# Attention with product features and a multiplicative FFN on one core: the end of the first query quarter in halves, the first keys' maximum in three parts, and a new order of all steps

## The chip, the core and the metric

One core of a Trainium2 chip runs the whole program: TensorE (PE) multiplies, VectorE (DVE), ScalarE (ACT) and GpSimd (POOL) do the rest, and SyncE (SP) issues nearly all DMAs, ACT a few. The metric is the device time of one execution in microseconds.

## The reference

For 4 batches of 4 heads with 1088 rows of 32 numbers, keys and queries are mapped to 64 products each (8 sketches times 8 sketches), attention is computed without a softmax, and its 4352 rows of 128 numbers go through a feed-forward block with two products multiplied:

```python
def phi(x):
    a = np.einsum('rd,bhsd->bhsr', S1, x)
    b = np.einsum('rd,bhsd->bhsr', S2, x)
    return np.einsum('bhsi,bhsj->bhsij', a, b).reshape(*x.shape[:-1], r * r)
q_p, k_p = (phi(q), phi(k))
kv = np.einsum('bhsf,bhsd->bhfd', k_p, v)
z = np.sum(k_p, axis=2)
num = np.einsum('bhsf,bhfd->bhsd', q_p, kv)
den = np.einsum('bhsf,bhf->bhs', q_p, z)[..., None] + 1e-06
...
x = attn_out.transpose(0, 2, 1, 3).reshape(B * S, H * D)
a = x @ w1
b = x @ w2
h = a * b @ w3
out = h @ w_out
```

The sketches and the FFN weights arrive as 64-bit floats and are converted on the chip from their two words. `w3 @ w_out` is formed once ("fold"), so the last two products become one.

## The kernel before

The program is a set of named steps, each a small function that issues one or a few instructions, and a hand-written string `ORDER` that says in which order they are called. Each engine executes its own instructions in that order, so `ORDER` is the queue of every engine at once, SP's and ACT's DMA queues among them. `POOL` and `ACTS` name the steps that run on POOL or ACT where a choice exists; otherwise they run on DVE. `SLOTS` says which buffer of a kind each allocation takes, in the order of the allocations; an allocation waits until its buffer's last user is done.

The steps by their prefixes:

- `s.*`: the two sketches: loaded (`s.load`), put together from their words on ACT (`s.words`), scaled (`s.pair`) and split into a coarse part and a rest (`s.lead`, `s.sum`, `s.rest`), transposed, spread.
- `k0` to `k3`: the keys of one batch: loaded, their maximum (`max`, L569) gives a grid (`g`), on which they are split in `lead` and `rest`; `gram` forms their Gram matrix on PE; `Gm` to `N1` derive bounds and products from it, `ab` the sketches of the keys, `kp` their 64 products, `kv` the sums with the values; `kq` and `kz` bring these into the form that the queries use. `kr0`, `kr1` are the last 64 rows of two batches each. `v*.load` loads the values.
- `q0` to `q6`, `qr`: queries. `q0` and `q1` are the first two blocks of 512 rows, `q2` and `q3` the next two, `q4` and `q6` blocks of 1024, `qr` the 256 last rows of the batches. A block is transposed (`tr`), split, multiplied with the sketches (`A0`, `C0`, `A1`, `C1`), its products corrected (`sm`, `st`, `sh`, `sl`, `sc`), the denominators formed (`p01`, `p2`, `p12`, `dn`, `de`, `rc`), the products written out (`phi`), transposed on PE or DVE (`pt`, `pT`), multiplied with `kz` or `kq` (`x`) and copied to `xT`, the FFN's input. Only `q0` divides at the very end: `xs` (L1198) multiplies with the reciprocals, `xt` (L1206) transposes on PE, `xT` (L1213) copies on ACT.
- `w0` to `w10`: weights: loaded, and converted from words by ACT (`c`, `m`), DVE (`j`) and POOL (`a0`, `a1`). `w0` is the first half of the columns of w1 and w2, `w1` the second, `w2` is w_out, the rest are row blocks of w3. `f*` folds one block of w3 with w_out.
- `g0` to `g7`, `gr`: the FFN of 512 rows (`gr`: the 256 last): for each of 8 column blocks c a product with w1 (`a`, L1448), its copy on ACT (`c`, L1453), a product with w2 (`b`, L1458), their product on DVE (`m`, L1464), and the accumulation with the folded weights (`o`, L1471; for `gr` in two banks `o0`, `o1`, L1478). Then the result is brought back (`oT`) and stored (`st`): four stores on SP for each of g0 to g7 (L1426), one on ACT (`gr.st0`) and one on SP (`gr.st1`) for `gr` (L1432).
- `warm*`: matmuls of zeros that nobody reads (`idle_ps`, L221), 72 in all, and `c.act`, a copy of one number on ACT early on.

PE's instructions stand as `ORDER` has them. Near the end, the last group's accumulations alternate between the two banks, with `gr.oT0` and `gr.st0` ahead of the last of the second bank.

Of the kernel before, what the change touches and what calls it, by code (L numbers as in the profile page):

```python
# [66 lines left out]
k1.lead0 k1.tr1 warm23 q0.A0 warm15 w1.load kr0.ab warm4 warm12 kr0.abc k1.rest0 q1.l2 warm13 warm7 warm18 q0.C0 k0.N0
kr0.kp w1.m v0.load q0.sma q0.C0t q0.sta k0.N1 k0.kv0 k0.kv3 k1.gram0 k1.gram1 k0.kv1 q1.l1 k0.kv2 kr1.load v0.loadr
k0.kvr s.RC k0.Na warm10 warm21 kr1.tr k0.kvc k0.kvm q0.sha q0.sla k0.Nb k2.zero k0.Nh w0.load warm17 k1.tr0 kr1.kT
q0.sca k1.kT1 k1.kT0 k0.kzt q1.A0 k0.kz q0.A1 kr1.ab q0.al q0.phi0 q0.phi1 q1.sm q0.smy q0.sty q1.st q0.pt0 warm5  # L70
k0.kqt k0.Nl warm20 k0.Nf w0.m kr1.abc q0.pc0 q0.pt1 q0.shy q1.rm q0.C1 k1.gram2 k1.gram3 k1.gram4 q0.pc1 warm19 q0.x0
q1.load k0.Nr q0.sly q0.C1t q0.x1 w0.c q0.scy q0.p01 q0.p2 q1.sh q0.p12 q0.dn s.KS w0.j q1.C0 q0.de q1.sl q0.rc q0.xs
q0.xt q0.xT k1.ab w0.a1 v1.zero k2.load k2.loadr k2.max w1.c warm24 w0.a0 warm22 g0.3a q1.sca q1.p01 g0.3c k2.g
v1.loadr k1.Gm k2.lead0 q1.scy q1.al w2.load q1.p2 q1.p12 k1.abt q1.restT q1.dn g0.1a g0.3b w1.j q1.de k0.kq q1.rc
k1.Gt g0.3m q1.bs g0.2b w1.a0 q1.phi g0.0a g0.5a g0.4a q1.pt0 g0.0c w2.c g0.1c w3.load w2.m k2.rest0 q1.pt1 g0.6a
g0.2a q1.pc0 w2.j k1.Ga k1.kp0 q1.pc1 g0.5c g0.2c g0.6c k2.gram0 q2.tr k1.Gb k1.T0 k2.gram1 k1.T1 q2.max k1.Ta k1.Tb
k1.Ts w2.a0 w4.load q1.x w1.a1 k2.gram2 k2.gram3 k2.gram4 k1.N0 k1.N1 s.AR warm16 k2.Gm q1.xT g1.7a q2.l2 k2.Gt k2.Ga
g0.6b g0.0b w3.c q2.l1 k1.Na k1.Nb k1.Nr k2.Gb w4.m g0.4c g0.6m g0.1b g0.7a g0.0m q2.rm w4.c q2.C0 q2.A0 q2.C1 g0.1m
w4.j w3.j g1.7c warm28 g0.7c w3.m g1.4a g1.2a g0.7b q3.tr q2.Ct g0.2m g1.6a q2.At g1.6c w4.a0 w3.a0 g1.1a g1.7b
q2.load q3.max q4.tr w6.load v1.load w2.a1 w4.a1 g1.2c f1.t g0.7m w3.a1 g1.1c w6.c q3.l2 g1.5a g1.7m q3.l1 q2.sm f0.t  # L80
g1.3a g0.4b f1.m w9.load warm27 f0.m q2.st q2.sh q4.max f0.o q2.sl g1.5c g0.4m q2.sc f1.o g1.3c g1.2b q2.p01 q3.rm
v2.zero k1.kp1 q2.al q2.p2 q2.p12 g1.2m k1.kv0 k2.T0 k1.kv2 k1.kv3 k2.T1 k1.kv1 k1.kvr q3.C0 q3.A0 q3.C1 w5.load
k1.kvc g1.4c k1.kqt k2.Ta k2.Tb q2.dn k2.Ts q2.de w6.j q2.rc g1.0a q3.Ct q2.bs g1.3b g1.6b g1.5b g1.3m q2.phi0 q3.At
w6.m g0.5b w5.m w5.c g1.5m g1.1b g1.0b g1.6m q3.sm g0.0o w9.c k1.kq w9.m g0.1o g1.0c k2.N0 k2.N1 q2.pT0 g0.5m q2.x0
g1.0m q3.st g1.1m q2.restT warm11 k3.zero w6.a0 k2.Na q3.sh w7.load kh2.load w6.a1 q3.sl w9.j k2.Nr w5.j q2.xT0 g1.4b
w9.a0 w9.a1 w5.a0 f3.t g1.0o q3.load g2.6a w10.load k3.loadr g2.6b g1.1o g2.1a g2.6c q4.l2 q4.l1 w7.m g2.1c w7.c g2.6m
g1.4m k2.Nb f6.t f3.m q3.sc g2.3a g2.7a g2.7c f3.o g2.3c q3.p01 q3.al k2.kT1 w5.a1 q3.p2 q3.p12 q3.dn k2.kT0 q4.rm
f6.m f6.o w10.c w8.load k2.ab w8.c q4.C0 q4.A0 q4.C1 w7.j k2.abt warm9 g2.4a f2.t q4.Ct g1.6o g2.0a f2.m g2.2b k3.load
q4.At q4.sm q3.de w7.a0 g2.0c f2.o v2.loadr w7.a1 kh3.load g0.2o f4.t q3.rc w10.m f4.m g2.2a k2.kp0 g0.6o f4.o q3.bs
w8.m w8.j g1.3o w8.a0 v2.load q3.phi0 g2.2c g2.4c w10.j q3.pT0 q3.x0 w8.a1 g0.3o q3.xT0 g2.7b w10.a0 w10.a1 k2.kp1  # L90
f5.t k3.max q6.tr f5.m g3.0b k3.kT1 g2.7m q3.restT f7.t g3.0a f5.o g3.0c g3.0m g3.3a g0.5o g3.3c g2.1b g2.2m g3.4a
g1.4o g1.5o k3.kT0 q6.max k3.g g2.1m g3.4c g2.5b f7.m f7.o g1.2o g2.0b q4.st q4.sh k3.lead0 q4.sl g3.7a g1.7o g3.7c
k3.rest0 kr1.kp q4.sc q4.al k2.kv0 k2.kv3 k2.kv1 k2.kv2 k3.ab k2.kvr k3.gram0 k3.gram1 k3.gram2 k3.gram3 k3.gram4
k2.kvc q4.p01 k2.kqt q4.p2 g2.0m k3.abt k3.Gm g0.4o g2.5a q4.p12 g2.5c k2.kq q4.dn q4.de k3.Gt g2.5m g3.6b g2.4b g2.0o
g3.6a q4.rc g3.6c k3.Ga q4.bs g1.oT g2.4m q4.phi0 q4.phi1 q4.pT0 k3.Gb g0.7o g3.4b g3.4m v3.zero k3.kp0 v3.load
v3.loadr g3.3b g2.4o g2.3b g2.3m g3.6m q4.pT1 g0.oT qr.max g3.2a g3.1a g2.6o g2.5o g3.2b g2.3o g3.3m k3.kp1 g3.1c
g3.2c qr.l2 k3.T0 k3.T1 k3.Ta g3.2m q4.x0 q4.x1 k3.kv0 k3.kv1 k3.Tb k3.N0 k3.kv3 k3.kv2 k3.kvr k3.Ts q6.l2 q6.l1 k3.N1
q6.rm k3.Na q4.xT0 warm6 k3.Nr k3.Nb q4.xT1 g4.2a g2.2o g5.2a g4.2c q6.C0 q6.A0 k3.kvc q6.C1 g5.2c q6.At q6.Ct q6.sm
k3.kqt g2.1o g4.3a g3.0o g5.4a g4.0a g2.7o g5.3a q6.st g4.0c g5.4c g5.3c g4.3c q6.sh q6.sl g5.0a q6.sc q6.p01 q6.al
q6.p2 q6.p12 g5.3b g2.oT g5.3m q6.dn g5.4b g5.7a q6.de k3.kq q6.rc qr.l1 qr.rm q6.bs q6.phi0 q6.phi1 g5.4m g5.1a  # L100
q6.pT0 g3.1b g5.1c g3.5a g5.7b g3.5c g5.0c g5.7c g3.1m q6.pT1 g3.4o g3.5b g3.3o q6.x0 q6.x1 q6.xT1 q6.xT0 g5.1b g5.7m
g5.1m g3.5m g5.0b g6.6a g3.7b g5.0m g3.7m qr.C0 g6.6c qr.A0 qr.C1 qr.At warm25 g6.0b g6.0a g6.0c g6.0m qr.Ct qr.sm
g5.2b g7.4a g4.1a g6.5a g4.4a g4.4c g4.1c qr.st qr.sh qr.sl g3.1o g5.2m g7.2a g3.6o g3.2o g4.5a g3.5o g4.5c g7.2c
g7.0a g4.4b g5.0o g5.1o g5.5a g5.2o g7.0c g7.4c g5.5c g6.2a qr.sc g4.4m qr.al g7.6a g6.4a g6.2c g6.5c g6.4c g5.6a
qr.p01 g5.6c g7.5a g6.7a g7.6b g7.5c g5.4o g6.2b g7.6c g7.0b g5.6b g5.5b g6.7c g6.2m g4.0b g7.4b g5.3o g5.5m g5.6m
g7.5b g6.4b g7.4m g5.5o qr.p2 g7.6m g6.1a g5.6o g3.7o g4.2b qr.p12 g4.0m g7.0m g7.5m g6.7b qr.dn g4.6b g6.5b g6.7m
# [1458 lines left out]
```

## Time and profile before

| what | value |
|---|---|
| median of 3 runs | 254.68 us (254.6 to 254.73) |
| the profiled run's own time | 254.37 us |
| its span, first to last instruction | 252.6 us |
| granted clock of TensorE | 1.0 |
| busy: PE, DVE, ACT, POOL | 246.1, 160.0, 99.7, 66.8 us |
| DMA traffic | 22.01 MB |

The span begins with the first instruction and ends with the last; the run's time has 1.77 us more around it. Busy time of PE includes fillers and the pipeline's run-out, so a share of 97% does not say that it did useful work for all of it. A line of a timeline begins with its start in us and its length in us; instructions of one kind that follow each other are merged, their length reaching to the end of the last.

### The profile page before, as it was taken

To read this page: it belongs to the slowest core of one execution; us is meant where nothing else is said; L and a number is where in the kernel's file an instruction comes from. 1 tells how busy PE (TensorE), PEld (TensorE's weight loads), DVE (VectorE), ACT (ScalarE), POOL (GpSimd) and SP (SyncE) were. 2 spreads that over 40 slices of the span, in tenths; PEclk is the share of its full clock that TensorE was granted. 3 is DMA by queue.
4 is the path that set the end of the run, shared out by engine and by line. 5 is a ranking of instruction groups with operands and counts; after the bars stand their busy time and mean duration, and the time that the engine had idled before them with its cause. 6 is when DMAs were issued, how large, how long until landed. Compare 5 with 4: busy or idle time off the path is not lost.

```text
span 252.6 us, 5980 instructions
## 1 busy us (share of the span) xinstructions
PE 246.1 (97%) x2503; PEld 137.9 (55%) x2503; DVE 160.0 (63%) x358; ACT 99.7 (39%) x183; POOL 66.8 (26%) x99
## 2 busy tenths in 40 slices
PE   8799999999999999998999999999999999999994
PEld 6689845457456576456446444444444444456554
DVE  2999998989998995938677597550115371424040
ACT  4588398763918543340225143213340012211010
POOL 4644535393546309203540016010000001000000
PEclk9999999999999999999999999999999999999999
DMA  6867793996679930200000000000000007205014
GB/s 182 262 173 263 222 241 84 259 254 139 160 206 235 249 90 0 85 6 3 3 0 3 3 0 1 4 0 0 3 0 0 0 2 123 44 0 83 0 28 76
DMA packets 31130, 22.01 MB, mean 87 GB/s; under 512 B 21248, under 2 KB 25600, under 8 KB 30976
## 3 DMA queue, kind: packets, MB, share of 16 engines
q1 hardware_dynamic: 30416, 21.05, 33.9%
q10 hardware_dynamic: 688, 0.59, 0.7%
q8 instruction: 19, 0.31, 0.5%
q14 instruction: 7, 0.06, 0.1%
HBM read 19.40 MB, written 2.23 MB: 86 GB/s over the span
## 4 chain that ended last, share of the span: by engine, by line
PE 95%; issue 1%; DMA 1%; POOL 1%; ACT 1%; DVE 0%; SPq 0%; POOLq 0%; ACTq 0%
PE a_ps L1448 23%; PE b_ps L1458 23%; PE ps_o L1471 22%; PE ps_w3o L478 6%; PE ps_g L604 3%; PE ps_x L1408 2%; PE idle_ps L221 2%; PE ps_ac L1294 2%; PE ps_kv L714 2%; PE ps_or L1478 1%; DMA s_raw<-in_S_dram 1%; PE ps_ab L672 1%; PE ps_ab L647 1%; PE ps_xt L1195 1%; PE ps_kt L630 1%
## 5 line engine op out<-in xcount | busy, mean ns | idle before, releaser
L1464 DVE TENSOR_TENSOR ab<-ffa,b_ps 128x512 f32<-128x512 f32 (+1 forms) x72 | 44.9, 649 | 60.8 <-PE b_ps L1458 40.9
L1453 ACT COPY ffa<-a_ps 128x512 f32<-128x512 f32 (+1 forms) x72 | 38.6, 566 | 96.4 <-PE a_ps L1448 93.8
L1448 PE MATMUL a_ps<-xT,w 128*128 128x512 f32 (+1 forms) x144 | 66.7, 570 | 0.0
L1458 PE MATMUL b_ps<-xT,w 128*128 128x512 f32 (+1 forms) x144 | 65.5, 569 | 0.0
L1471 PE MATMUL ps_o<-ab,w3o 128*128 128x512 f32 x128 | 62.3, 594 | 0.0
L1448 PEld LDWEIGHTS a_ps<-xT,w 128*128 128x128 f32 x144 | 26.5, 190 | 30.0 <-issue 23.9
L1458 PEld LDWEIGHTS b_ps<-xT,w 128*128 128x128 f32 x144 | 26.9, 190 | 29.1 <-issue 25.0
L1471 PEld LDWEIGHTS ps_o<-ab,w3o 128*128 128x128 f32 x128 | 23.9, 190 | 25.5 <-issue 24.0
L442 POOL TENSOR_TENSOR w3c<-cv_c,cv_m 128x512 int32<-128x512 int32 x16 | 20.8, 1333 | 22.0 <-DVE cv_c L431 13.7
L1389 POOL TENSOR_TENSOR ph<-s_al,s_bs 128x1024 f32<-128x1024 f32 (+1 forms) x6 | 10.8, 1808 | 52.7 <-DVE s_bs L1379 52.7
L478 PEld LDWEIGHTS ps_w3o<-wo,w3T 128*128 128x128 f32 x128 | 15.4, 192 | 3.6 <-issue 3.3
L478 PE MATMUL ps_w3o<-wo,w3T 128*128 128x128 f32 x128 | 15.6, 275 | 0.0
L221 PE MATMUL idle_ps<-zeros 128*128 128x256 bf16 x72 | 13.3, 317 | 1.0 <-DVE zeros L193 1.0
L229 ACT ACTIVATE cv_c<-raw 128x1024 f32<-128x1024 f32 x11 | 12.8, 1175 | 2.1 <-DMA raw<-in_moe_w_dram 2.1
L417 ACT ACTIVATE cv_m<-raw 128x1024 int32<-128x1024 uint32 x11 | 12.8, 1178 | 0.0
L472 DVE STREAM_TRANSPOSE w3T<-w3c 128x1024 f32<-128x1024 f32 x8 | 9.8, 1230 | 3.5 <-POOL w3c L442 3.5
L604 PE MATMUL ps_g<-kk 128*32 128x64 f32 x288 | 8.2, 225 | 2.1 <-POOL kk L596 1.1
L1346 POOL TENSOR_TENSOR s_al<-s_hl 128x128 f32<-128x128 f32 (+2 forms) x3 | 2.3, 753 | 29.7 <-DVE s_hl L1341 29.7
L1419 ACT COPY xT<-ps_x 128x128 f32<-128x128 f32 (+2 forms) x20 | 4.6, 325 | 13.1 <-PE ps_x L1408 9.5
L1397 DVE STREAM_TRANSPOSE pT<-ph 128x1024 f32<-128x1024 f32 (+1 forms) x7 | 8.2, 1164 | 2.5 <-POOL ph L1389 2.4
L221 PEld LDWEIGHTS <-zeros 128*128 128x128 bf16 x72 | 7.5, 114 | 3.9 <-issue 1.0
L604 PEld LDWEIGHTS ps_g<-kk 128*32 128x32 f32 x288 | 7.0, 109 | 2.8 <-POOL kk L596 1.2
(241 smaller groups left out, 284.3 us busy)
## 6 DMA issues: line engine op xcount, KB each, us to landing
raw<-in_moe_w_dram SPq DMA_DIRECT2D x32, 256.0 KB, 7.6
qh<-in_q_dram SPq DMA_DIRECT2D x4, 544.0 KB, 3.5
out_dram<-oT SPq DMA_DIRECT2D x33, 64.0 KB, 2.0
raw<-in_moe_w_dram SPq DMA_DIRECT2D x4, 512.0 KB, 5.8
k<-in_k_dram SPq DMA_DIRECT2D x3, 512.0 KB, 5.9
v<-in_v_dram SPq DMA_DIRECT2D x2, 512.0 KB, 6.4
raw<-in_moe_w_out_dram SPq DMA_DIRECT2D x1, 1024.0 KB, 6.0
kh<-in_k_dram SPq DMA_DIRECT2D x8, 128.0 KB, 6.3
```

Of the source, the lines that this page charges most:

```text
L221: pe.matmul(t, zeros, bview(zeros, [[0, 2], [1, 128]]), start=True, stop=True)
L229: act.activation(dst, hi.bitcast(F32), ACT.Prelu, scale=2.0 ** -112, alpha=-2.0 ** 32)
L417: act.mul(x["m"], words(0).bitcast(U32), 2.0 ** -29)
L442: pool.tensor_tensor(d, c, m, ALU.add)
L478: pe.matmul(t["o"], w3T[ko][:, c], wo[:, c], start=c == 0, stop=c == NC - 1)
L604: pe.matmul(o[h * D:(h + 1) * D], lhs, rhs, start=start, stop=stop, skip_group_check=True)
L1389: on(nm(f"phi{u}")).tensor_mul(x, bview(s["al"][:, u * g], [[r, g], [1, r], [0, r]]), bview(s["bs"][:, u * g], [[r, g], [0, r], [1, r]]))
L1448: pe.matmul(x["a"][:, :w], w_of(0, c), xT[g][:, c0:c0 + w], start=True, stop=True)
L1453: act.copy(x["s"][:, :w], x["a"][:, :w])
L1458: pe.matmul(x["b"][:, :w], w_of(1, c), xT[g][:, c0:c0 + w], start=True, stop=True)
L1464: dve.tensor_mul(ab_sb[g, c][:, c0:c0 + w], x["s"][:, :w], x["b"][:, :w])
L1471: pe.matmul(o_ps[g], w3o[:, c], ab_sb[g, c], start=c == 0, stop=c == NC - 1)
```

## The change

- `HALVES` cuts column blocks 0 and 1 of `g0` into halves of 256 rows (`g0.0aa` is the first half's product with w1, `g0.0ba` the second's).
- The end of `q0` (`xs`, `xt`, `xT`) is done in halves of 256 rows.
- The maximum over the first keys is taken in three parts: heads 0 and 1, heads 2 and 3, and the column of last rows for all heads; a fourth number holds the maximum of the first two.
- `rm`, `sca`, `scy`, `sc`, `p01` and `bs` may now run on POOL, and `POOL` names another set of steps: among others `k0.kp1`, `k1.kp0`, `k2.kp0`, `k3.kp1`, `k2.rest0`, `k3.rest0`, `q1.phi`, `q3.phi0` and the corrections of `q0` come to POOL, `k0.rest0`, `k0.rest1`, `s.low`, `s.sum`, `q0.phi1`, `q2.phi0`, `q4.phi0`, `q4.phi1`, `q6.phi0`, `qr.phi0` leave it for DVE.
- The store of the second bank of `gr` is cut in two: 16 of the 32 row groups on SP (`st1`), 16 on ACT (`st2`).
- `ORDER` and `SLOTS` are new throughout. `k1.zero` and `k1.load` take the buffer of the first keys (slot 0 of kind `x`) and come after the Gram products of `k0`; `k2.zero` stands near the start. `c.act` stands near the end, `warm25`, `warm20` and `warm28` behind everything.

The beginning and the end of the new order, and the other edits:

```diff
+HALVES = ((0, 0), (0, 1))
...
 ORDER = """
-s.load k1.zero c.ident c.mask k0.zero c.zeros warm0 k0.loadr k0.load0 k0.load1 c.act s.words s.pair s.lead q0.load
-k0.max0 k0.max1 k0.g k0.lead0 warm1 k1.loadr s.low s.sum s.four k0.tr0 k0.lead1 s.rest s.T k0.kT0 k0.rest0 warm8 q0.tr
...
-gr.5o0 gr.1o0 gr.4o0 gr.0o1 g4.oT gr.6o1 gr.5o1 gr.3o0 g6.oT g4.st g6.st gr.1o1 gr.2o0 gr.7o0 gr.4o1 gr.oT0 gr.3o1
-gr.2o1 gr.7o1 gr.st0 gr.oT1 gr.st1
+c.zeros c.ident s.load s.four warm13 k0.zero warm12 warm10 warm9 warm7 k0.load0 k0.loadr k0.load1 q0.load k2.zero
+c.mask s.words k0.max0 kr0.load k0.max1 s.pair k0.max2 s.lead s.low k0.g k0.lead0 warm1 k0.tr1 k0.tr0 warm0 s.sum
...
+gr.1b g7.4o g2.st g7.2o gr.1m g7.7m gr.3m g7.3o g7.1o g7.7o gr.0o1 gr.6o1 gr.6o0 gr.5o0 g7.oT gr.1o0 gr.5o1 gr.1o1
+gr.4o1 gr.3o1 gr.2o1 g7.st gr.7o1 gr.4o0 gr.3o0 gr.2o0 gr.7o0 gr.oT0 gr.oT1 gr.st2 gr.st1 gr.st0 warm25 warm20 warm28
 """
...
-            for i in range(2):
+            for i, (h0, h1, j0, j1) in enumerate(((0, 2, 0, NJ), (2, H, 0, NJ), (0, H, NJ, NK))):
                 @step(f"k{b}.max{i}")
-                def _(i=i):
+                def _(i=i, h0=h0, h1=h1, j0=j0, j1=j1):
                     if i == 0:
-                        g["m"] = sb("k_m", [128, 2])
-                    peak(g["m"][:, i:i + 1], k_sb[b][:, 2 * i:2 * i + 2].rearrange("p h j d -> p (h j d)"))
+                        g["m"] = sb("k_m", [128, 4])
+                    peak(g["m"][:, i:i + 1], k_sb[b][:, h0:h1, j0:j1].rearrange("p h j d -> p h (j d)"), AX.XY)
+                    if i == 1:
+                        dve.tensor_max(g["m"][:, 3:], g["m"][:, :1], g["m"][:, 1:2])
...
-            @step(nm("xs"))
-            def _():
-                s["xs"] = sb("t2", [128, nj, H * D], name="xs")
-                dve.tensor_mul(s["xs"].rearrange("p j (h d) -> p (j h) d", d=D),
-                               s["x"].rearrange("p j (h d) -> p (j h) d", d=D),
-                               bview(s["rc"], [[1, nj * H], [0, D]]))
...
+            for u in range(2):
+                cut_j = slice(2 * u, 2 * u + 2)
+
+                @step(nm(f"xs{u}"))
+                def _(u=u, cut_j=cut_j):
+                    if u == 0:
+                        s["xs"] = sb("t2", [128, nj, H * D], name="xs")
+                    dve.tensor_mul(s["xs"][:, cut_j].rearrange("p j (h d) -> p (j h) d", d=D),
+                                   s["x"][:, cut_j].rearrange("p j (h d) -> p (j h) d", d=D),
+                                   bview(s["rc"][:, 2 * u * H:], [[1, 2 * H], [0, D]]))
...
-    def rest_dst(oT, u):
-        (sp if u else act).dma_start(bass.AP(tensor=out.tensor, offset=(NT - 2 + u) * DM,
-                             ap=[[NT * DM, 32], [S * DM, B], [1, DM]]), oT)
+    def rest_dst(oT, u, t0=0, n=32):
+        (sp if u and not t0 else act).dma_start(bass.AP(tensor=out.tensor, offset=(NT - 2 + u + t0 * NT) * DM,
+                             ap=[[NT * DM, n], [S * DM, B], [1, DM]]), oT[t0 * B:(t0 + n) * B])
...
-                step(f"g{g}.st{u}")(lambda u=u: dst(z[u], u))
+                if u == 0:
+                    step(f"g{g}.st0")(lambda: dst(z[0], 0))
+                else:
+                    for i in range(2):
+                        step(f"g{g}.st{1 + i}")(lambda i=i: dst(z[1], 1, 16 * i, 16))
```

More of the change, by code (lines that the diff above doesn't have):

```diff
@@ L48 @@
 BY_PE = ()
+HALVES = ((0, 0), (0, 1))
 QUARTERS = (0, 2, 1, 3)
 POOL = set("""
-    k0.Nh k0.rest0 k0.rest1 k1.kp1 k2.kp1 k3.kp0 q0.phi1 q1.al q1.p12 q1.p2 q2.al q2.p12 q2.p2 q2.phi0
-    q3.p2 q4.al q4.p12 q4.phi0 q4.phi1 q6.p12 q6.phi0 q6.phi1 qr.al qr.p2 qr.phi0 s.Pp s.blk s.blkh
-    s.low s.rest s.sum
+    k0.Nf k0.Nh k0.Nl k0.kp1 k1.kp0 k1.kp1 k2.kp0 k2.kp1 k2.rest0 k3.kp0 k3.kp1 k3.rest0 q0.p01 q0.p12
+    q0.p2 q0.sca q0.scy q1.phi q2.al q2.bs q2.p01 q2.p12 q2.p2 q2.sc q3.p01 q3.p12 q3.p2 q3.phi0 q3.sc
+    q4.al q4.p01 q4.p12 q4.p2 q6.al q6.p01 q6.p12 q6.phi1 q6.sc qr.sc s.Pp s.blk s.blkh s.rest
 """.split())
@@ L67 @@
[L67 to L106, printed above, removed]
@@ L112 @@
[L112 to L114 removed]
+c.zeros c.ident s.load s.four warm13 k0.zero warm12 warm10 warm9 warm7 k0.load0 k0.loadr k0.load1 q0.load k2.zero
+c.mask s.words k0.max0 kr0.load k0.max1 s.pair k0.max2 s.lead s.low k0.g k0.lead0 warm1 k0.tr1 k0.tr0 warm0 s.sum
+k0.lead1 q0.tr kr0.tr s.rest warm18 k0.rest0 s.T s.tc k0.gram0 s.R k0.gram1 k0.rest1 k0.gram2 k0.gram3 k0.gram4 s.zero
@@ new lines @@
+q1.C0 q0.sly q0.C1t k0.kvm q0.phi0 k0.Nr k0.kzt k2.load q0.phi1 k1.kT0 k0.kz q0.pt0 k1.rest0 q1.A0 warm8 q1.sm kr1.tr
+q0.pc0 q0.pt1 w0.load q0.x0 q0.pc1 w0.c q1.st q0.scy q0.p2 q0.p12 q1.load q0.dn q0.x1 q1.sh q0.de w0.j q0.rc k1.gram0
+q0.xs0 q0.xs1 k1.gram1 k1.gram2 k1.gram3 w0.m q1.sl k1.gram4 warm19 k1.Gm k0.kvc q0.xt0 q1.restT q1.sca k2.max w0.a0
+q0.xt1 w0.a1 warm16 q1.p01 q1.scy k1.Gt warm5 warm17 warm6 s.AR q1.al q1.p2 q1.p12 q1.dn w1.c q0.xT0 q1.de g0.0aa
+q0.xT1 g0.3a g0.2a kr1.kT g0.2c g0.0ac w1.m g0.3c w2.load s.KS k1.Ga k2.g w1.j g0.3b g0.0ab w1.a0 g0.2b g0.0ba k1.T0
@@ new lines @@
+w10.load g2.0m w8.a1 q3.x0 q3.xT0 w5.m f4.t f5.t g2.1a g1.6o warm11 g2.1c k3.lead0 g2.1b g2.3b w5.a0 w5.a1 g2.3m f2.t
+g2.7m g2.4b f5.m kh3.load f5.o w10.m f2.m f2.o w10.c w6.a0 g3.6a q4.sh g3.3a g0.1o w6.a1 f3.t q6.tr w10.j f3.m g3.7a
+k3.kT0 k2.kp1 g2.1m f4.m w10.a0 g3.3c g3.7c f3.o q4.sl g0.2o g0.6o warm27 g0.3o warm26 g0.5o q4.sc k3.rest0 k2.kp0
+g2.4m q4.al q4.p01 q4.p2 kr1.kp k3.gram0 f4.o k3.gram1 k2.kv0 k2.kv3 k2.kv1 k2.kv2 k3.gram2 k2.kvr k3.gram3 w10.a1
+k3.gram4 k3.kT1 k3.ab q4.p12 q4.dn q3.restT k2.kvc k2.kqt k2.kq g3.1a g2.0o g0.4o k3.Gm k3.abt v3.zero f7.t g2.6b
```

117 lines of the change are left out of this document (74 added, 43 removed).

## The prediction

> **What bounds the kernel now.** I read the page's busy shares first, then the chain that ended last in order of time, then each engine's timeline where the chain changes character, and at the end the waits of SP's queue.
>
> ```profile
> span 252.6 us, 5980 instructions
> PE 246.1 (97%) x2503; PEld 137.9 (55%) x2503; DVE 160.0 (63%) x358; ACT 99.7 (39%) x183; POOL 66.8 (26%) x99
> PE   8799999999999999998999999999999999999994
> DVE  2999998989998995938677597550115371424040
> ```
>
> PE is busy throughout, yet not always with work: 62 of its 72 `idle_ps` matmuls (L221, filler) start before 30.3 us. The chain shows where the filler ends:
>
> ```profile
> 29.08 0.44 PE ps_xs L1209 x4
> 29.52 0.60 PE ps_ab L672 x32
> 30.11 0.33 PE idle_ps L221 x2
> 30.44 1.80 PE a_ps L1448 x4
> ```
>
> From the first FFN product at 30.44 on, the 128x512 products follow each other at 0.86 us, and PE is busy 79.57 of the 79.60 us from 30.4 to 110. So there are three places where this change can move the end: the start of that dense stream, holes torn into it, and what follows its last matmul. Before 30 us DVE is the limit: it is busy 22.11 of the 23.10 us from 5.6 to 28.7. The end looks like this (timeline, then chain):
>
> ```profile
> 243.96 4.61 SPq L1426 DMA_DIRECT2D out_dram<-oT  x8
> 248.55 0.27 ACT L1498 COPY oT<-ps_or 128x128 f32<-128x128 f32 x1 [6.75 <-PE ps_or L1478]
> 248.85 0.64 ACTq L1432 DMA_DIRECT2D out_dram<-oT  x1
> 249.45 0.29 DVE L1498 COPY oT<-ps_or 128x128 f32<-128x128 f32 x1 [2.85 <-PE ps_or L1478]
> 249.77 0.62 SPq L1432 DMA_DIRECT2D out_dram<-oT  x1
> ```
>
> ```profile
> 245.84 3.58 PE ps_or L1478 x32
> 249.42 0.02 issue
> 249.45 0.29 DVE oT L1498
> ```
>
> PE ends at 249.42. One copy and one store follow, on SP, issued at 249.77; from that issue to the end of the span it is 2.83 us. PE's end to the span's end: 3.18 us. ACT's store was out 0.9 us earlier, and all of SP's eight earlier stores were issued by 248.57.
>
> **Part 1, the last stores: +3.75 us.** The last accumulations are reordered: bank 1 of the rest rows ends four products before bank 0, so the copy on DVE (`gr.oT1`) is early, and the copy on ACT (`gr.oT0`) waits for the last matmul. The second bank's store is cut in two: `gr.st1` on SP, `gr.st2` on ACT. Behind ACT's copy stand, in its order, `gr.st2` and `gr.st0`. What decides is a wait that the diff doesn't show. DMAs take eight completion counters in turn, and a DMA is issued only when the one before it on its counter has landed. In the built order of the changed kernel ACT's two stores are numbered ahead of SP's last stores: the second of the four stores of group 7 waits on the counter that `gr.st2` raises, the third on that of `gr.st0`, and SP issues in order, so the fourth and `gr.st1` stand behind them. In the order of before, ACT's only store has a counter that no later store uses. That such a wait holds SP is in the waits of SP's queue, on weight loads that waited for weight loads:
>
> ```profile
> SPq L402 <- DMA raw<-in_moe_w_dram: 3.4, 5, 1.0
> DMA to landing us min/median/max: 2.0/2.0/2.0
> ```
>
> (The second line is of the two stores at L1432.) From PE's end T: ACT's copy is done at T+0.30 (0.27 and 0.03 to the issue, as at 248.55), `gr.st2` issues at T+0.33 and lands 2.0 later, T+2.33. Group 7's second, third and fourth store take 0.577 each (4.61 for eight): T+4.06. The third also needs `gr.st0`, issued at T+0.97 (0.64 behind `gr.st2`) and landed at T+2.97, 0.06 later than the second store is out: T+4.12. There `gr.st1` issues, and 2.83 later the span ends: T+6.95. Less 3.18 this is +3.77; I take +3.75. Ends: +2.7, if stores issue at their fastest (0.316) and land in 1.8, the fastest of L1426; +3.9, if each of the three takes 0.64, the slowest issue there. Nothing hides it, PE has finished; the three fillers placed behind the last product lie beside it.
>
> **Part 2, up to the first FFN product: +0.3 us.** The maximum in three parts lets DVE start when `k0.load0` lands. That load is issued at 0.75, and the fastest landing at L504 is 2.8, so 3.6 instead of 5.63. But `q0.tr` is next to wait: the first query load (issued at 2.30, landing 5.4, the largest of L909) lands at 7.7, and DVE began `q0.tr` at 7.80 before. So the head start of 2.0 us stops there: in it lie `s.pair` (0.68), the third maximum (0.2), the scale, `k0.lead0` (0.46) and the two small sketch steps taken from POOL. `c.act` moving to the end makes ACT load its table (1.28) behind the sketch's DMA (3.72) instead of before it, so `s.words` comes at 5.0 instead of 3.79; DVE takes `s.pair` at 5.45 anyway, behind the maxima, so it costs nothing; without that cover it would be 1.2.
>
> From `q0.tr` to the end of `xs` DVE had 20.9 us (7.80 to 28.70). Behind it now come off: `k0.kp1` to POOL (1.15), `k0.Nf/Nl` (0.20), `q0.sca` (0.32), `scy` (0.21), `p01` (0.34), `p2` (0.20), `p12` (0.31), and `q1.sl` and `s.KS` to later (0.43): 3.16. There come on: `k0.rest0` (0.58, by 128x512 at DVE's rate of 1.15 per 1024) and `rest1` (0.70) from POOL, `q0.phi1` (0.61), `xs` in two (0.09): 1.98. Net -1.2, so 7.7+20.9-1.2=27.4. New waits: `rest1` for ACT's `k0.lead1` (0.15), `P_g` behind ACT's order (0.3), `q0.al` for POOL's `sca` (0.5): 28.35. `k1.load` reuses the first keys' buffer and is issued only at about 11.1, after the Gram products (SP's `v0.load` to `w0.load` stand behind it); `v0.load`, of the same size, was used by 18.63 having been issued at 12.71, so at most 5.9 later: 17.0, against its maximum at 16.4; I cost it 0, up to 0.6. ACT then has `pc1`, two weight conversions (1.16 and 1.18), a third (1.16) and only then `xT0`, so the first product comes some 0.75 after `xs`, at 29.1. By then PE has not done `k1.ab` (0.60), `k0.kqt` (0.22) and `kr1.ab` (0.26), which it did before 30.44: 29.1+1.08-30.44=-0.26. The halves themselves cost PE nothing (two times 0.43 for 0.86, as `gr` shows), DVE 0.06 each.
>
> Against this stands what POOL and DVE do to each other:
>
> ```profile
> 17.45 1.78 POOL L785 TENSOR_TENSOR kpr<-krab 128x256 f32<-128x256 f32 x1 [3.57 <-DVE kp L622]
> 101.91 0.63 POOL L785 TENSOR_TENSOR kpr<-krab 128x256 f32<-128x256 f32 x1
> 40.95 0.48 DVE L170 SCALAR_TENSOR_TENSOR T_p<-T_g,T_t 32x32 f32<-32x32 f32 x1
> ```
>
> The same multiplication takes POOL 1.78 beside DVE's 1.27 us subtraction at 17.38 and 0.63 elsewhere; DVE's `T_p`, 0.18 elsewhere, takes 0.48 beside a POOL addition. The change puts POOL's `sca`, `p01`, `scy`, `p2`, `p12` (about 0.46 each, `p01` 0.73) beside DVE's `al`, two `phi` and `k1.rest` (0.61 to 1.27), in alternating dependence; two such collisions are worth 1.15 by the row. That makes +0.9. Between -0.26 and +0.9 I take +0.3; ends -1.3 (no new wait at all) and +1.5.
>
> The Trainium skill, SBUF — State Buffer, section Who interferes with whom, says that a DVE instruction with both inputs in SBUF and a GpSimd instruction that reads SBUF exclude each other for a whole instruction, the later one waiting. The trace agrees (1.78 against 0.63). By that rule the front would be at +0.9 rather than -0.26, and it speaks against this change.
>
> **Part 3, inside the dense stream: +0.1 us.** POOL gets `k1.kp0`, `k2.kp0` and `k3.kp1` (1.95 each), `k2.rest0` and `k3.rest0` (2.8 each: 1.28 and 1.56 for 512 and 640) and small steps of q2 to q6 (some 7 by 0.46 for 128 columns); two `phi` come and three go (1.96): some 16 us on its 37.1 busy us of 79.6, so it has room. DVE loses about 7 there, which gains nothing, as PE is full. Nearest to a hole is `k2.gram0`: POOL must first add `w1.a0` (to 34.3), `q1.phi` (1.96) and `w1.a1` (1.27) and then subtract `k2.rest0` (to 40.2), and PE runs out of queued products at about 39.75: +0.45. Three fillers of 0.11 leave for the end: -0.3. I round to +0.1; ends -0.3 and +2.0 (each of the six moved POOL steps late by 0.35).
>
> **Sum.** 0.3+0.1+3.75=+4.15: span 256.75, the profiled run 254.37+4.15=258.5. The median before is 0.31 above the profiled run, so on it 258.8. I say 258.6.
>
> **Rivals.**
> (a) POOL and DVE collide all the way: the front at +0.9 and, by the 1.15 lost at 17.45, one more collision in the dense stream, +1.2: 254.68+0.9+1.2+3.75-0.3=260.2. For it: the rows above; against it: POOL idle for half of that time. This is what the skill's rule named above would make of the time.
> (b) The front gains all it can (-1.3, and no hole: -0.3), the end is held: 254.68-1.3-0.3+3.75=256.8. For it: DVE has 3.16 us less; against it: three named waits.
> (c) The other side: the end is not held. Place: group 7's second store. If SP issues it before ACT's stores have landed, the end is `gr.st0` alone, behind `gr.st2`, at the fastest issue rows (0.316): T+0.65+2.83, +0.3 instead of +3.75. With the front at its queue sum (-0.26) and the fillers gone (-0.3): 254.68-0.26-0.3+0.3=254.4. It decides as soon as that store starts before T. Against it: the waits in the built order, and SP's 3.4 us above.
>
> **Chances.** Forecast 0.58 (own range 257.6 to 259.6), (a) 0.18, (b) 0.14, (c) 0.10. The range 256.5 to 260.6 leaves out (c) and a little of the ends of (a) and (b). Within 0.2% (0.5 us) is what a measurement can hardly tell from no change. Faster comes from (c) alone, 0.06; same from the rest of it, 0.03; slower 0.91.
>
> **What would show it.** In the changed profile: PE's last `ps_or` near 249.8, with three fillers behind it; ACT's copy right after it, two ACT stores; then SP stores at L1435 starting 2 us after PE's end, waiting for the DMA of `out_dram`, and the store of `gr.st1` last, near 253.9. The first `a_ps` near 29.1 with `k1.ab` behind it; the first `k_m` near 3.6, DVE idle before `qT` until 7.7. The prediction is wrong if SP's stores don't wait at the end, if the first `a_ps` lies outside 28 to 31, or if PE has holes of over 2 us between 30 and 110.

## The result, and the profile after

The changed kernel takes 256.04 us (median of 4 runs, 255.94 to 256.25), the kernel before 254.64 beside it (254.57 to 254.73): ratio 1.0056, 95% interval 1.0038 to 1.0073. It is slower by 1.4 us. The direction is the one forecast, the size is not: 258.6 was said, and the range began at 256.5.

The head of the changed kernel's page (span; busy tenths of PE and DVE in 40 slices) and its packets of instructions:

```profile
span 254.2 us, 6032 instructions
PE   8899999999999999999999999999999999999990
DVE  4899898999999969647839584523073144531310
q8 instruction: 20, 0.33, 0.6%
```

PE is as full as before and ends earlier; no matmul starts in the last slice any more. The chain that ended last, around the first FFN product (start, us, what):

```profile
28.15 0.77 PE ps_xs L1218 x4
28.92 0.66 PE idle_ps L223 x6
29.58 2.24 PE a_ps L1458 x6
```

The first `a_ps` is 0.86 us earlier than before (29.58 against 30.44). The end, first as a chain, then as a timeline of SP's queue (start, us, engine, line, operation), then as a timeline of ACT and SP from 246 us on (with what the engine waited for), where the last three of SP's four stores have a row of their own, then the waits of SP's queue from 246 us on (total, times, longest):

```profile
239.97 4.29 PE ps_o L1481 x10
244.26 3.35 PE ps_or L1488 x30
247.60 0.33 PE idle_ps L223 x3
```

```profile
245.04 6.19 SPq L1435 DMA_DIRECT2D out_dram<-oT  x4
251.32 0.61 SPq L1441 DMA_DIRECT2D out_dram<-oT  x1
```

```profile
247.64 0.27 ACT L1508 COPY oT<-ps_or 128x128 f32<-128x128 f32 x1 [18.48 <-PE ps_or L1488]
247.70 1.31 ACTq L1441 DMA_DIRECT2D out_dram<-oT  x2
249.61 1.62 SPq L1435 DMA_DIRECT2D out_dram<-oT  x3
```

```profile
SPq L1435 <- DMA out_dram<-oT: 4.7, 2, 4.2
```

PE's last product ends at 247.60, 1.8 us earlier than before. Group 7's first store goes out at 245.04, the other three only from 249.61 on: SP stood 4.2 us waiting for a DMA on `out_dram`. In the trace `gr.st2` lands at 249.59 and `gr.st0` at 250.36, and SP's second and third store start at 249.61 and 250.38. The last store, `gr.st1`, issues at 251.32, 3.72 us after PE's end.

| us | before | after | difference |
|---|---|---|---|
| first `a_ps` | 30.44 | 29.58 | -0.86 |
| from it to PE's last product | 218.98 | 218.02 | -0.96 |
| from there to the span's end | 3.18 | 6.59 | +3.41 |
| span | 252.6 | 254.2 | +1.6 |

So the end lost 3.4 us, near the forecast, and ahead of it 1.8 us were gained where the forecast has a loss of 0.4, though the dense stream now also holds 1.08 us of work that lay ahead of it before. To see where, I took from the trace the time from each matmul's start to the next one's, by what they write, between the first `a_ps` and PE's end:

| us | `ps_g` | `ps_x` | `ps_kv` | fillers | `ps_or` | `a_ps`, `b_ps` | `ps_ab`, `ps_kq`, `ps_krab` |
|---|---|---|---|---|---|---|---|
| before | 5.04 | 7.21 | 3.67 | 1.16 | 3.73 | 117.90 | 2.01 |
| after | 3.74 | 6.79 | 3.31 | 1.03 | 3.57 | 118.25 | 2.93 |

The largest difference is in the Gram products `ps_g`, 288 in both. It is a hole of the kernel before, in the chain of its Gram products:

```profile
115.85 1.64 PE ps_g L604 x79
117.48 0.99 issue
118.47 0.28 PE ps_g L604 x3
```

"issue" says that PE waited for nothing that the profile shows. The windows around it (PE's, PEld's, DVE's, ACT's and POOL's busy time with instructions, granted clock, DMA share, GB/s) show one transfer:

```profile
116.10:117.10 1.00, 1.00 (x108) 1.00 (x99) 0.47 (x2) 0.19 (x1) 0.50 (x1) 1.00 0.06 16
117.10:117.48 0.38, 0.38 (x34) 0.27 (x21) 0.38 (x1) 0.00 (x0) 0.34 (x1) 1.00 0.00 0
117.48:118.47 0.99, 0.01 (x1) 0.00 (x0) 0.87 (x3) 0.00 (x0) 0.39 (x1) 1.00 0.00 0
```

16 GB/s for 1 us is one packet of 16 KB, and it is one of the queue "q8 instruction". The changed kernel's PE has no such wait; its Gram products there pass straight into the sketches of the keys:

```profile
110.54 0.54 PE ps_g L608 x24
111.08 0.59 PE ps_ab L676 x16
111.68 0.37 PE ps_kq L754 x2
```

That this packet is what PE waits for was my theory from here on.

### The profile page after: what moved, and what is told of

Read it like the earlier page. It is cut to its first block, busy times and chain, and to the rows that moved or that the text cites. A ratio compares the mean times of both kernels' runs of the same rounds, so it can differ in the third digit from the quotient of the medians.

```text
span 254.2 us, 6032 instructions
## 1 busy us (share of the span) xinstructions
PE 245.7 (97%) x2511; PEld 140.1 (55%) x2511; DVE 159.2 (63%) x351; ACT 100.3 (39%) x186; POOL 82.3 (32%) x111
## 4 chain that ended last, share of the span: by engine, by line
PE 87%; DVE 5%; DMA 2%; POOL 2%; issue 1%; SPq 1%; DVEq 0%; POOLq 0%
PE a_ps L1458 23%; PE b_ps L1468 23%; PE ps_o L1481 22%; PE ps_w3o L480 6%; PE ps_x L1417 2%; PE ps_g L608 2%; PE ps_ac L1303 2%; DMA qh<-in_q_dram 2%; PE ps_or L1488 1%; PE ps_kv L718 1%; POOL RC L345 1%; PE idle_ps L223 1%; PE ps_ab L676 1%; DVE k_m L182 1%; PE ps_kq L754 0%
## 5 line engine op out<-in xcount | busy, mean ns | idle before, releaser
L1474 DVE TENSOR_TENSOR ab<-ffa,b_ps 128x512 f32<-128x512 f32 (+1 forms) x74 | 45.9, 636 | 44.2 <-PE b_ps L1468 34.7
L1468 PE MATMUL b_ps<-xT,w 128*128 128x512 f32 (+1 forms) x148 | 67.4, 560 | 0.0
L1481 PE MATMUL ps_o<-ab,w3o 128*128 128x512 f32 x128 | 60.8, 595 | 0.0
L1458 PEld LDWEIGHTS a_ps<-xT,w 128*128 128x128 f32 x148 | 27.1, 190 | 27.6 <-issue 22.1
L1497 DVE STREAM_TRANSPOSE oT<-ps_o 128x512 f32<-128x512 f32 x8 | 5.7, 713 | 18.7 <-PE ps_o L1481 18.7
L1350 POOL TENSOR_TENSOR s_hl<-s_hl,ay_C 128x256 f32<-128x256 f32 (+2 forms) x4 | 3.2, 794 | 37.1 <-DVE s_hl L1346 25.8
L626 POOL TENSOR_TENSOR kp<-kabt 128x1024 f32<-128x1024 f32 x6 | 12.1, 2028 | 1.9 <-DVE kabt L694 1.2
L1398 POOL TENSOR_TENSOR ph<-s_al,s_bs 128x1024 f32<-128x1024 f32 x2 | 5.1, 2560 | 9.2 <-DVE s_bs L1388 9.2
```

The costliest lines, as they stand in the source:

```text
L626: eng.tensor_mul(dst, bview(av, [list(av.ap[1]), list(av.ap[2]), [0, r]]), bview(bv, [list(bv.ap[1]), [0, r], list(bv.ap[2])]))
L1458: pe.matmul(x["a"][:, :w], w_of(0, c), xT[g][:, c0:c0 + w], start=True, stop=True)
L1468: pe.matmul(x["b"][:, :w], w_of(1, c), xT[g][:, c0:c0 + w], start=True, stop=True)
L1474: dve.tensor_mul(ab_sb[g, c][:, c0:c0 + w], x["s"][:, :w], x["b"][:, :w])
L1481: pe.matmul(o_ps[g], w3o[:, c], ab_sb[g, c], start=c == 0, stop=c == NC - 1)
```

## The experiments

Each time stands beside runs of the kernel before on the same chip.

**e1_all_stores_sp.** All rest stores on SP's queue.

```diff
-        (sp if u and not t0 else act).dma_start(
+        sp.dma_start(
```

> The changed kernel with its three rest stores all on SP (st2 and st0 taken from ACT); PE's order, the copies and the cut of the second bank are as they were. Theory (ACT's two stores hold SP's queue through shared completion counters): in the built order no store of SP now waits on one of ACT's, group 7's stores go out as soon as its transpose is done (245.0), and only gr.st0 follows the copy of ACT: PE's end plus 0.33 for its issue plus 2.83, a tail of 3.2 us instead of 6.6. Span 250.8, time 256.04 - 3.4 = 252.6. Rival (the tail is long because three stores are issued one behind the other after a late copy): SP issues seven stores after the transpose of group 7 instead of five, so the tail stays over 5.5 us, time 255 to 257.

Measured: 253.47 us, ratio 0.9954 (0.9938 to 0.9970). PE's end to the span's end is 3.85 us. SP's stores no longer wait for a DMA, and the three rest stores follow each other (the stores' wait from 240 us on; timeline):

```profile
SPq L1435 <- DVE oT L1497: 2.4, 1, 2.4
```

```profile
248.57 1.92 SPq L1441 DMA_DIRECT2D out_dram<-oT  x3
```

With the cut store SP has six issues of 0.5 to 0.6 behind group 7's first, and `gr.st0` goes out 0.93 after PE's end, not 0.33. The hold is the cause of the long end; the rest of 0.6 is SP's queue, as e5 shows. (The profiled run of this kernel has its first `a_ps` 1.4 us later than the others, because PE waited 1.73 us for a load of the rest keys; from 10.63 to 14.04 it also had half its clock, see the last section.)

**e2_only_st0_on_act.** Only `gr.st2` moves to SP.

```diff
-        (sp if u and not t0 else act).dma_start(
+        (sp if u else act).dma_start(
```

> The changed kernel with st2 moved to SP and st0 left on ACT. Theory (hold by counters): in the built order the third store of group 7 now waits on the counter that st0 raises. st0 issues 0.33 after PE's end and lands 1.9 later, at PE's end + 2.25; the third and fourth store of group 7 and st1 take 0.5 to 0.6 each, so st2 issues at +3.9 and the span ends at +6.7: the tail is as long as in the changed kernel (6.6), time 256.1, although ACT issues one store instead of two. Rival (the cost lies in the number of stores on ACT or in the cut): some 0.6 us less than the changed kernel, 255.4, or the whole gain of the kernel with all stores on SP, 252.6.

Measured: 256.28 us, ratio 1.0073 (1.0051 to 1.0095), no gain at all. The timeline of its end, and SP's wait:

```profile
248.00 0.64 ACTq L1441 DMA_DIRECT2D out_dram<-oT  x1
250.01 0.85 SPq L1435 DMA_DIRECT2D out_dram<-oT  x2
250.96 1.25 SPq L1441 DMA_DIRECT2D out_dram<-oT  x2
```

```profile
SPq L1435 <- DMA out_dram<-oT: 3.9, 1, 3.9
```

The wait has moved from the second to the third store of group 7, where the built order has it, and that store starts at 250.01, when `gr.st0` lands (250.00). One store on another queue is enough to hold SP's queue.

**e3_new_end_on_before.** The end of the changed kernel (bank 0 last, cut store, two stores on ACT) on the kernel before.

```diff
...
-gr.2o1 gr.7o1 gr.st0 gr.oT1 gr.st1
+gr.2o0 gr.7o0 gr.oT0 gr.oT1 gr.st2 gr.st1 gr.st0
...
-        (sp if u else act).dma_start(
+        (sp if u and not t0 else act).dma_start(
```

> The kernel before with the end of the changed kernel alone: bank 0 of the rest rows ends last, the second bank's store is cut in two, st2 and st0 on ACT. In its built order the counters of ACT's two stores are not taken up again by any store of SP, since SP has one store fewer behind them. Theory (hold by counters): no hold; SP is through when ACT copies, and the end is st0 behind st2 on ACT, 0.97 + 2.83 = 3.8 us after PE's end against 3.18: time 254.64 + 0.6 = 255.3. Rival (the new order of the end and the cut cost 3.4 by themselves): 258.0.

Measured: 255.49 us, ratio 1.0027 (1.0010 to 1.0044): +0.6. Its span ends 3.86 us after PE's last product, at 249.52. All of SP's stores are issued before ACT's two (timelines of SP and ACT):

```profile
248.97 0.62 SPq L1432 DMA_DIRECT2D out_dram<-oT  x1
```

```profile
249.61 1.32 ACTq L1432 DMA_DIRECT2D out_dram<-oT  x2
```

The same edit costs 3.4 us where a later store of SP takes ACT's counter again, and 0.7 where none does.

**e4_fillers_fewer.** 16 idle matmuls fewer in the first 8 us of the kernel before.

```diff
-WARM = [16, 10, 6] + ...
+WARM = [7, 3, 6] + ...
```

> The kernel before with 16 of its 72 idle matmuls taken out, all of them in the first 8 us, where PE has nothing else to do. Theory (the 0.99 us hole of before at 117.48 is PE's instruction supply: a 16 KB instruction packet starts at 116.15, when 3322 of PE's instructions have started, PE runs through 168 more in a burst of short matmuls and then stands until 2.3 us after that start): 32 instructions fewer ahead of it move the packet some 32 instructions later into the burst, PE reaches the end of the burst (6 instructions behind the hole) before it runs out, and the long products cover the rest. The hole goes: time 254.64 - 1.0 = 253.65. Rival (the hole is a wait for data or is there in any case): the 16 idle matmuls lie beside other engines' work, so no change, 254.6.

Measured: 255.21 us, ratio 1.0013 (0.9997 to 1.0030): no gain, yet the hole is gone. From the first `a_ps` to PE's end it is 217.91 us instead of 219.12 (here and below from the start of the first matmul itself, 30.29 in the kernel before and 29.43 in the changed one, where the chain says 30.44 and 29.58), `ps_g` 3.82 instead of 5.04. The gain was lost ahead of it: the first `a_ps` came 1.85 us later. The timeline of PE shows why:

```profile
1.00 2.32 PE L221 MATMUL idle_ps<-zeros 128*128 128x256 bf16 x10 [1.00 <-DVE zeros L193]
...
7.21 1.46 PE L221 MATMUL idle_ps<-zeros 128*128 128x256 bf16 x6
```

The six at 7.21 take 0.24 each. In the kernel before, where PE had been busy without a break to 6.7, six at 7.07 take 0.14 each (0.83 together): without the fillers PE was still at its slow rate, and the first Gram products with it. (The trace of this run records the full clock only from 13.75 us on, that of the kernel before from 5.46.) My theory of the hole held, the rest of the expectation fell.

**e5_sp_uncut.** As e1, and the second bank's store in one piece.

```diff
-                    for i in range(2):
-                        step(f"g{g}.st{1 + i}")(lambda i=i: dst(z[1], 1, 16 * i, 16))
+                    step(f"g{g}.st1")(lambda: dst(z[1], 1))
```

> The changed kernel with the rest rows' two stores on SP and the second bank's store in one piece again (the kernel with all stores on SP had 15 and 3 stores, this one has 15 and 2). Theory (what is left of the tail beyond 3.2 is SP's queue: with the cut, st0 could issue only at PE's end + 0.87 behind group 7's four stores and the two halves, 0.6 each): st0 issues at PE's end + 0.33, tail 3.2 instead of 3.85, 0.6 less than with the cut: ratio to the kernel before 0.993, some 252.8 to 252.9. Rival (that run's longer tail is the landing of its last store): no difference, 253.5.

Measured: 252.59 us, ratio 0.9898 (0.9870 to 0.9926). PE ends at 247.60 as in the changed kernel; the timeline of the end:

```profile
247.41 1.30 SPq L1441 DMA_DIRECT2D out_dram<-oT  x2
...
247.64 0.27 ACT L1508 COPY oT<-ps_or 128x128 f32<-128x128 f32 x1 [18.49 <-PE ps_or L1488]
```

The tail is 3.30 us. This beats the kernel before by 2.4 us and the changed kernel by 3.3 (spans) to 3.9 us (each against the runs of the kernel before beside it). The next kernels start from it.

**e6_rc_later.** POOL's `s.RC` behind `q0.p12`.

```diff
-... q0.sca q0.p01 s.RC q0.al ... q0.scy q0.p2 q0.p12 ...
+... q0.sca q0.p01 q0.al ... q0.scy q0.p2 q0.p12 s.RC ...
```

> As e5_sp_uncut, and POOL's three copies of s.RC, which stood between p01 and scy of the first query quarter, put behind its p12. In the changed kernel they took 2.65 us beside DVE's two phi products and key scaling; the same three copies took 0.61 in the kernel before. Theory (POOL and DVE hold each other up at this place, and POOL's copies stand ahead of scy, p2 and p12, for which DVE's s_d waits 0.8 us): scy starts some 1 to 2 us sooner, DVE's wait of 0.8 goes, the first a_ps and all behind it come 0.8 us earlier: 252.0. Rival (the collision goes with the place: p2 and p12 get slower beside the same DVE work, or PE and ACT end the wait instead): 0 to 0.3 us.

Measured: 252.70 us, ratio 0.9902 (0.9878 to 0.9926), the same. The three copies in the kernel before and in the changed one, then the timeline of POOL in this run:

```profile
19.18 0.49 POOL L343 COPY RC<-Sc 128x32 f32<-128x32 f32 x3
```

```profile
21.80 2.65 POOL L345 COPY RC<-Sc 128x32 f32<-128x32 f32 x3
```

```profile
23.39 0.87 POOL L1111 TENSOR_TENSOR s_pr<-s_al,s_loy 128x128 f32<-128x128 f32 x1
24.34 1.46 POOL L1115 TENSOR_TENSOR s_pr<-s_pr 128x128 f32<-128x128 f32 x1
25.74 0.50 POOL L345 COPY RC<-Sc 128x32 f32<-128x32 f32 x3
```

The copies are short again (0.50 for 2.65), and DVE's wait of 0.8 is gone, but `p2` and `p12` now take 0.87 and 1.46 where they took 0.46 each. The first `a_ps` is at 29.64 against 29.43. The rival held: here the steps that stand beside DVE's long products are slow, whichever they are.

**e7_small_steps_on_dve.** `q0.sca`, `scy`, `p01`, `p2`, `p12` taken out of the set `POOL`, so that DVE does them.

> As e5_sp_uncut, with five small steps of the first query quarter (sca, scy, p01, p2, p12) back from POOL to DVE: the change's move undone for the quarter whose end starts the FFN. The prediction's sum has 1.38 us of DVE time gained by the move, against it 0.9 for collisions and 0.5 for a wait, together about nothing: by it the first a_ps stays within 0.3 us and so does the time. Rival 1 (the collisions cost nothing, the move gains what it takes from DVE): 1.4 us slower than e5. Rival 2 (POOL and DVE lose more to each other than the prediction has it): 0.5 to 1.5 us faster than e5.

Measured: 252.73 us, ratio 0.9904 (0.9880 to 0.9928), first `a_ps` at 29.80 against 29.43. The move of these steps is worth 0.1 to 0.4 us: about nothing, as the sum had it.

**e8_fillers_fewer_later.** 11 idle matmuls fewer in the kernel before, after PE's rate is full.

```diff
-WARM = [16, 10, 6] + [4] * 2 + [2] * 8 + [1] * 16
+WARM = [16, 10, 6] + [1] * 2 + [1] * 5 + [2] * 3 + [1] * 16
```

> The kernel before with 11 idle matmuls taken out again, not in the first 8 us this time but after PE has reached its full rate (its matmuls take 0.27 us from 5.5 us on), one of them in the dense stream. In e4_fillers_fewer the hole at 117.48 went as the theory of PE's instruction supply says, and PE's dense stretch was 217.9 instead of 219.1, but 16 matmuls fewer at the start left PE at half rate (0.42 instead of 0.27) up to 11 us, and the front lost 1.75. Theory: 22 instructions fewer move the packet far enough, the hole goes and the front stays: 1.2 us less than before, ratio 0.995. Rival (the fillers hold PE's rate here too): dense stretch 217.9, but the front later by 0.5 or more.

Measured: 253.13 us, ratio 0.9941 (0.9916 to 0.9966). The chain where the hole was:

```profile
115.79 1.68 PE ps_g L604 x80
117.47 0.37 PE ps_kq L750 x2
117.84 0.86 PE ps_o L1471 x2
```

First `a_ps` where it was (30.30 against 30.29), dense stretch 217.72 instead of 219.12. Leaving out 22 of PE's instructions, which do no work, takes 1.5 us (by the ratio) from the kernel before: it was carrying a hole that goes when PE has a few instructions fewer ahead of it.

**e9_no_halves.** `g0.0` and `g0.1` whole again (their first halves' steps do nothing, the second ones do all 512 rows).

> As e5_sp_uncut, with the two column blocks of the first group's products (g0.0, g0.1) whole again: one product of 512 rows where the change has two of 256. The prediction has it that the halves cost PE nothing (2 x 0.43 for 0.86) and that the end of the front is not worth more for them. Theory: the first product now waits for the second half of xT, 0.2 to 0.3 later than 29.43, and PE's dense stretch loses the 0.35 that a_ps and b_ps together have more in the changed kernel than before (59.34 + 58.91 against 59.15 + 58.75): within 0.2 us of e5. Rival (the halves bring the front forward by more, since PE and ACT alternate at the start): 0.5 us or more slower than e5.

Measured: 253.41 us, ratio 0.9941 (0.9927 to 0.9956). First `a_ps` 29.70 against 29.43, dense stretch 218.40 against 218.18; `b_ps` has 0.11 less, not 0.35 with `a_ps`. The halves are worth 0.3 (spans, 251.2 against 250.9) to 1.1 us (ratios), more than I gave them.

**e10_table_load_first.** `c.act` back at the start.

> As e5_sp_uncut, with c.act, ACT's first instruction that loads its table, back at the start. The prediction costs its move to the end at nothing, with DVE's maxima as the cover: by it the sketch words come 1.2 us sooner and DVE still begins s.pair at 5.2 to 5.4, the query's transpose still waits for its load (7.2 to 7.5), no change (0.1 us). Rival (the sketch's chain through ACT and POOL ends later waits, at P_g or Sc): up to 0.7 us faster.

Measured: 252.81 us, ratio 0.9923 (0.9897 to 0.9950); profiled span 250.8 against 250.9, first `a_ps` 29.51 against 29.43. No difference to be told.

**e11_max_in_two.** The first keys' maximum in two parts, with the rest rows in each.

```diff
...
-            for i, (h0, h1, j0, j1) in enumerate(((0, 2, 0, NJ), (2, H, 0, NJ), (0, H, NJ, NK))):
+            for i, (h0, h1, j0, j1) in enumerate(((0, 2, 0, NK), (2, H, 0, NK))):
...
```

> As e5_sp_uncut, with the first keys' maximum in two parts again, each of which needs both loads of the keys: DVE starts near 5.6 instead of 3.5. The prediction has the head start of 2 us stop at the query's load (7.7) and then be used by some 1.3 us of work moved into it. Theory: without it that work (s.pair, the sketch steps, k0.lead0) lies behind the maxima, the query's transpose comes at 8.5 to 8.8 instead of 7.5, and the first a_ps 1.0 to 1.4 us later: 253.6 to 254.0. Rival (the head start is worth nothing, as other waits follow before the first product): 252.6.

Measured: 254.98 us, ratio 1.0001 (0.9986 to 1.0017), some 2.6 us more than e5, beyond what I expected. The first `k_m` starts at 5.85, the query's transpose at 8.78 (e5: 3.46 and 7.48). Only these early times are read from its profile, since PE got half its clock in that run from 11.8 us on (last section).

**e12_dense_fillers_out.** The 7 idle matmuls of the dense stream and the 3 at the end left out.

> As e5_sp_uncut, without the 7 idle matmuls inside the dense stream and the 3 behind the last product. The prediction counts a filler in the dense stream at 0.11 of PE's time. Theory: PE is full there, each filler is cost, 7 of them 0.8 us by the changed kernel's stretch (9 fillers 1.03): 251.8. Rival 1 (they stand where PE would wait anyway): 252.6, with holes where they were. Rival 2 (20 instructions fewer shift PE's instruction packets and a hole like that of before at 117.48 comes back): 252.8 or more.

Measured: 252.19 us, ratio 0.9890 (0.9876 to 0.9904), the fastest median; against e5 the intervals overlap. Dense stretch 217.50 against 218.18, no hole. In the profiled run 0.57 of that is given back, because PE waited 1.06 for the load of the rest keys (chain):

```profile
3.65 5.17 DMA kr<-in_k_dram
```

**e13_14_fillers_more, e14_28_fillers_more.** e5 with 14 and 28 idle matmuls more, near 43 and 72 us.

```diff
+WARM[15] += 7; WARM[23] += 7
```

(That is e13; e14 has 14 in place of each 7.)

> As e5_sp_uncut, with 14 idle matmuls more (28 of PE's instructions), 7 each near 43 and 72 us, ahead of the burst of short matmuls at 108 to 112. They cost PE 14 x 0.11 = 1.55, so PE's dense stretch is 218.18 + 1.55 = 219.7 if nothing else happens. Theory (whether the burst outruns PE's instruction supply is a matter of where the packets' edges fall in it): the edges lie 28 instructions earlier in the burst, about where they lay in the kernel before, whose burst ended 31 instructions later than that of the changed kernel; a hole of up to 1.2 us comes back behind the Gram products, dense stretch 220.2 to 220.9. Rival (the new order of the Gram products removed the hole): 219.7, no hole.

> As e13_14_fillers_more, with 28 idle matmuls more (56 of PE's instructions). They cost 3.1: dense stretch 221.3 if nothing else happens. Theory: the edges lie 56 instructions earlier, well inside the burst, so if the hole isn't there with 28 it is here, about 1 us, 222.0 to 222.5, and it lies further ahead in the burst than in e13 if it was there too. Rival (the new order removed it): 221.3, no hole.

Measured (one run each): 255.54 and 259.22 us. Dense stretches 221.26 and 224.86, so 1.5 and 3.6 more than the fillers' own time (1.53 and 3.06), and more than expected in both. The chains of e13 and e14:

```profile
112.05 0.54 PE ps_g L609 x24
112.59 0.58 PE ps_ab L677 x12
113.17 0.95 issue
```

```profile
115.65 0.51 PE ps_g L609 x22
116.16 1.43 issue
```

The hole is back in both. In e14 it lies 14 matmuls further ahead in the program (2 `ps_g` and 12 `ps_ab`), by as many as were added. Counted from PE's first, the matmul that waits is number 1741 in both, 1746 in the kernel before. Counted with weight loads and semaphore instructions, 3521 of PE's instructions have started ahead of the wait in all three, and in e3, where the hole also stands. PE stands at a fixed place of its instruction stream, and it shows when fast instructions reach that place. (e14 has a second hole of 1.74 at 64.2, after 2242 instructions; it isn't there in e5 and e13, which have fewer fillers near 43.) The rival, that the new order of the Gram products keeps the hole away whatever the count, is refuted. In the changed kernel itself the next instruction, number 3522, starts at 115.32, behind long products that follow the burst.

## Why the prediction was right and wrong

**Part 1, the last stores: right, 3.41 instead of 3.75.** The counters hold SP at just the two stores named; e2 and e3 show that it follows the counters, not the number of stores or the cut. The size was 0.34 too large. `gr.st2` issues 0.10 after PE's end, not 0.33: it doesn't depend on the copy of `gr.oT0`, and it goes out 0.06 after that copy starts (247.64 and 247.70). With it `gr.st0`, for which SP's third store waits, lands earlier, so that this store starts 2.78 after PE's end, not 2.97. The third and fourth store then take 0.94 together, not 1.15, and from the issue of `gr.st1` to the end it is 2.87, not 2.83.

**Part 2, the front: right, +0.22 instead of +0.3** (first `a_ps` 0.86 earlier, and 1.08 of work that was done ahead of it before). The first `k_m` starts at 3.56 (3.6 forecast), the query lands in time for the transpose at 7.25 (7.7), both halves of `xs` are through at 28.43 (28.35). DVE didn't sit idle ahead of the transpose: the sketch's small steps filled the time, and e11 shows that this head start is worth 1.3 us at the transpose. The moves of `c.act` (e10) and of the five small steps (e7) come to nothing, as costed. The collisions came at another place than I named, on `s.RC`: 2.65 us for three copies that took 0.49 before, so that the size of this part came out right is in part luck. The Trainium skill's rule that the prediction names (SBUF — State Buffer, Who interferes with whom) agrees with that and with e6, where the slowness goes to the steps that take their place. That the sum gives the halves nothing was too low (e9).

**Part 3, the dense stream: wrong, and this is the step that failed.** Forecast +0.1 with ends -0.3 and +2.0; measured -0.96 - 1.08 = -2.0. I asked only which new holes the change would make. The one I named, +0.45 at `k2.gram0`, didn't come: POOL ended `k2.rest0` at 40.88, even later than the 40.2 I had, but PE had products queued until 41.49. I never asked which holes of the kernel before would go, though its chain has "117.48 0.99 issue" in it: the sum has that term at nothing, without a reason. The Gram products lost 1.30 us, nearly all of it that hole, and e4, e8, e13 and e14 show that the hole hangs on how many instructions PE has run, so that an edit ahead of it that changes this number can move it, remove it or bring it back. The other 0.7 is made up of `ps_x` -0.42, `ps_kv` -0.36, `ps_or` -0.16, fillers -0.13 and the moved work done in 0.92 instead of 1.08, against +0.35 on `a_ps` and `b_ps` and +0.14 elsewhere. The 0.42 of `ps_x` lies in two of its five blocks of 64 products (0.98 to 0.82 and 1.72 to 1.46), whose last seven stand among other products in the new order. That this mixing is the cause, there or in `ps_kv`, wasn't tried, so 0.7 us of the miss have no cause shown.

**The rivals.** (a) and (c) are refuted: the front didn't get to +0.9, and the stores were held. (b) has nearly the time (256.8) for a wrong reason: the front didn't gain all it can. No case let PE's dense stretch get shorter by more than 0.3, so the range ended 0.5 above the result.

**The working.** Three of its figures are off, and none explains the miss. DVE's subtraction at 17.38 takes 1.36 us in the timeline, not 1.27. POOL's terms up to `k2.rest0` add to 40.3, not 40.2. The sum on the median is 258.8, and 258.6 was said without a reason.

## What to carry to other kernels

Before changing the end of a kernel, follow each completion counter of the last stores. Here a late store on one queue held another queue's early ones that took its counter next, and putting all of them on one queue, uncut, turned this change from 1.4 us lost into 2.4 us gained. When a trace shows an engine idle with no releaser, price its going away as well as new holes; it may depend on nothing but the instruction count. And test a version with a few empty instructions more or fewer before crediting or blaming an edit for a microsecond.

## What the hardware showed that I had not expected

**PE's instruction supply.** PE's instructions come in packets of 16 KB: 19 for its 5049 instructions in the kernel before, 20 for 5079 in the changed one. The thirteenth packet starts at 116.15, 111.64 and 115.09 in the kernel before, e13 and e14, and PE, which stands in a burst of short matmuls, goes on at 118.47, 114.12 and 117.59, 2.3 to 2.5 us later; in e14's second hole the packet starts at 63.30, and PE goes on 2.65 us later. In the twelve profiles without the hole PE reaches the same instruction only 3.3 to 5.9 us after the thirteenth packet's start, behind long products, two of which take 0.86, and there is no wait. That the packet is what PE waits for is inferred from this agreement of count and time; no view names it.

**PE's rate after idling.** The windows of e11's profiled run:

```profile
8.00:10.00 2.00, 0.51 (x4) 0.18 (x2) 1.96 (x6) 1.90 (x6) 0.72 (x2) 1.00 0.89 318
12.00:25.40 13.40, 13.36 (x169) 11.29 (x160) 8.60 (x30) 5.91 (x13) 5.27 (x11) 0.50 0.71 208
25.40:30.00 4.60, 4.60 (x122) 4.37 (x119) 4.16 (x12) 3.21 (x6) 2.70 (x5) 0.99 0.34 103
```

PE is busy 0.51 us between 8 and 10, and then has half its clock up to 25.4, though it is busy all that time. The Trainium skill (TensorE: Matmul & The Clock Gate, Part 1: The HAM clock gate) says that PE's clock is halved after an idle window of about 3.4 us and full again after at least one busy one. The traces agree on the half clock, but only in part on the lengths. In e11 the clock was lost though PE was busy 1.88 us of the last 3.41 before the change at 11.81, and it took 13.65 us of a busy PE to get it back. In e1's profiled run PE was busy 1.69 of the 3.42 us before the clock was lost at 10.63, and it came back after 3.41 us, at 14.04, as the page has it.
